# Attention in pairs of heads h and h+4, with q and k on 128 partitions and the order of every engine written out

## The chip, the cores and the metric

The program runs on one core of one Trainium2 chip. The metric is device time in microseconds (us), the median of several executions. Several chips were used; the kernel before took 374 to 383 us on them, so every version below is compared with runs of the kernel before on the same chip in the same rounds. A ratio is the mean time of one kernel's fast runs over the mean of the other's of the same rounds, so it is not quite the ratio of the medians that are quoted. A run counts as slow when it lies over 1.5% above the fastest of the same kernel.

## The reference

Sliding-window attention with a linear bias, then a mixture of eight experts in which each token goes to the expert named by its domain id. Sizes: 8 batches, 8 heads, 576 positions, head size 64, window 128; 4608 tokens of 512 features, experts 512 to 1024 to 512.

```python
def _attn_ref(q, k, v):                       # all (8, 8, 576, 64) float32
    scores = scale * np.matmul(q, k.transpose(0, 1, 3, 2))
    rel = pos[:, None] - pos[None, :]
    bias = slopes[:, None, None] * (-np.abs(rel))[None]
    mask = (rel >= 0) & (rel < 128)
    scores = np.where(mask, scores + bias[None], -1e9)
    # ... softmax over the last axis ...
    return np.matmul(attn, v)

def _moe_ref(x, domain_id, w1, w2):           # x (4608, 512), w1 (8, 512, 1024), w2 (8, 1024, 512)
    for e in range(8):
        m = domain_id == e
        out[m] = np.maximum(x[m] @ w1[e], 0.0) @ w2[e]

def reference(...):
    x = attn_out.transpose(0, 2, 1, 3).reshape(4608, 512)
    return _moe_ref(x, ...)
```

## The kernel before

The kernel has two parts. In attention, each batch is loaded, q and k are transposed on TensorE, scores are exponentiated on ScalarE, masked on VectorE, multiplied by v on TensorE, divided by their row sums on VectorE, and the finished 128-token rows are scattered by expert into a buffer in device memory (`x_srt`). A short routing step computes the scatter addresses from the domain ids. In the expert part (MoE), each expert's rows are loaded from `x_srt`, transposed and put through two matmuls. The MoE part cannot start before the last scatter of the last batch has landed, because any expert may own any row.

The parts that the change and the argument touch (cuts are marked with `...`):

```python
    PR, CR = 96, 6                                   # q, k: 96 partitions x 6 rows
    ...
    def load_w(e):                                   # 2 DMAs of one expert's weights, on GpSimd's queue
        w1e = wpl.tile([128, 4, FF], F16, name="w1e", tag="w1e")
        nc.gpsimd.dma_start(out=w1e, in_=moe_w1[e]...)
        w2e = wpl.tile([128, 8, DX], F16, name="w2e", tag="w2e")
        nc.gpsimd.dma_start(out=w2e, in_=moe_w2[e]...)
        return w1e, w2e
    ...
        def load_b(b):
            # q16, k16: [96, 8, 6*64]; q and k on GpSimd's queue (they are cast to fp16 on the way)
            for h0 in range(0, H, step):
                for (src, dst) in ((q, q16), (k, k16)):
                    nc.gpsimd.dma_start(out=dst[:, h0:h0 + step, :], in_=src[b, h0:h0 + step]...)
            # v: five tiles on SyncE's queue
            ...
        def stage_t(b, hp):                          # 2 heads: 12 transposes for q, 12 for k
            for (src, dst) in ((q16, qT), (k16, kT)):
                for c in range(CR):
                    for hh in range(2):
                        nc.tensor.transpose(pst[64*hh:64*hh+64, c*PR:(c+1)*PR],
                                            src[:, 2*hp+hh, c*D:(c+1)*D], ident[0:PR, 0:PR])
                ...
        def stage_s(b, h):                           # one head: 5 matmuls on one half of the rows
            d0 = 64 * (h % 2)
            for kt in range(NT):
                nc.tensor.matmul(ps[:, o:o + w], kT[d0:d0+64, kt*128:kt*128+128],
                                 qT[d0:d0+64, kt*128:kt*128+w], ...)
            # Exp on ScalarE, two masks on VectorE
            ...
        def stage_av(b, h, et):                      # 9 matmuls, reciprocal, one division
            ...
        def stage_out(b):                            # on GpSimd: 5 token copies, then 5 scatters
            ...
        for i, (b, h) in enumerate(units):
            et = stage_s(b, h)
            if i == 1:
                routing()
            if h == 2 and b + 1 < B:
                loaded[b + 1] = load_b(b + 1)
            if h == 2 and b == B - 1:
                ws.append(load_w(0))
            ...                                      # transposes two pairs ahead, v casts at h == 5
            if prev is not None:
                stage_av(*prev)
                if prev[1] == H - 1:
                    stage_out(prev[0])
            prev = (b, h, et)
    ...
        xs = [load_x(0, MT)]                         # MoE: expert 0's rows from x_srt, on SyncE's queue
        turn_x(*xs[0], MT)
        ws.append(load_w(1))
        for e in range(E):
            if e + 2 < E:
                ws.append(load_w(e + 2))
            ...
```

Here the framework's scheduler decides the order on each engine; the source order is only a wish. It moves the weights of the first three experts far forward, as the profile shows.

The softmax here doesn't subtract the row's maximum and nothing guards it: scores larger than these inputs give would overflow.

Of the kernel before, what the change touches and what calls it, by code (L numbers as in the profile page):

```python
# [10 lines left out]
F16 = mybir.dt.float16  # L11
F32 = mybir.dt.float32
I32 = mybir.dt.int32
I64 = mybir.dt.int64
ACTF = mybir.ActivationFunctionType
# [11 lines left out]
def kernel(  # L27
# [17 lines left out]
    PR, CR = 96, 6  # L45
    HP = H // 2
# [30 lines left out]
    cst = np.zeros((128, 64), np.float32)  # L77
    for (b, t), c in colof.items():
        cst[:, c] = b * S + t * 128 + np.arange(128)
# [11 lines left out]
    psX = ctx.enter_context(tc.tile_pool(name="psX", bufs=2, space=PSUM))  # L91
# [4 lines left out]
    cs = cpool.tile([128, 64], F32, name="cs")  # L96
    nc.sync.dma_start(out=mat, in_=mats_h.ap())
    nc.sync.dma_start(out=gm[:, :, 0:256], in_=gmask_h.ap())
    nc.sync.dma_start(out=cs, in_=cst_h.ap())
    ident = mat[:, 0, :]  # L100
    nc.gpsimd.tensor_copy(out=gm[:, :, 256:448], in_=gm[:, :, 0:192])
    nc.gpsimd.tensor_copy(out=gm[:, :, 448:512], in_=gm[:, :, 0:64])
# [9 lines left out]
    kTs = [cpool.tile([128, 640], F16, name=f"kT{i}") for i in range(3)]  # L112
    qTs = [cpool.tile([128, S], F16, name=f"qT{i}") for i in range(3)]
    ets = [cpool.tile([128, 1088], F16, name=f"et{i}") for i in range(3)]
# [13 lines left out]
    with tc.tile_pool(name="qk_pool", bufs=2) as qk_pool, \  # L128
         tc.tile_pool(name="v_pool", bufs=6) as v_pool, \
         tc.tile_pool(name="r_pool", bufs=4) as r_pool, \  # L130
         tc.tile_pool(name="rt", bufs=1) as rt:

        def load_b(b):
            q16 = qk_pool.tile([PR, H, CR * D], F16, name="q16", tag="q16")
            k16 = qk_pool.tile([PR, H, CR * D], F16, name="k16", tag="k16")
            step = 2 if b == 0 else 8
            for h0 in range(0, H, step):
                for (src, dst) in ((q, q16), (k, k16)):
                    nc.gpsimd.dma_start(
                        out=dst[:, h0:h0 + step, :],  # L140
                        in_=src[b, h0:h0 + step].rearrange(
                            "h (p c) d -> p h (c d)", p=PR))
            v32 = []
            for t in range(NT):
                n = SSZ[t]
                v32t = v_pool.tile([128, H, D], F32, name="v32", tag="v32")
                nc.sync.dma_start(  # L147
                    out=v32t[0:n],
                    in_=v[b, :, t * 128:t * 128 + n, :].rearrange("h p d -> p h d"))
                v32.append(v32t)  # L150
            return q16, k16, v32

        loaded = {0: load_b(0)}

        for t in kTs:
            nc.vector.memset(t[:, S:640], 0.0)
        for t in ets:
            nc.gpsimd.memset(t[:, 1024:1088], 0.0)
# [7 lines left out]
        def routing():  # L166
# [28 lines left out]
            pp = psX.tile([128, 512], F32, space=PSUM, name="pp", tag="x")  # L195
            nc.tensor.matmul(pp[:, 0:E * NCOL], mat[:, 1, :], cf, start=True, stop=True)
            pt = psX.tile([128, 512], F32, space=PSUM, name="pt", tag="x")
# [61 lines left out]
        qkT = {}  # L259
        scat = []  # L260

        def stage_t(b, hp):
            q16, k16, _ = loaded[b]
            i = b * HP + hp
            qT, kT = qTs[i % 3], kTs[i % 3]
            for (src, dst) in ((q16, qT), (k16, kT)):
                pst = psT.tile([128, 1024], F16, space=PSUM, name="pst", tag="t")
                for c in range(CR):
                    for hh in range(2):
                        nc.tensor.transpose(  # L270
                            pst[64 * hh:64 * hh + 64, c * PR:(c + 1) * PR],
                            src[:, 2 * hp + hh, c * D:(c + 1) * D],
                            ident[0:PR, 0:PR])
                o = dst[:, 0:S].rearrange("p (r c) -> p r c", c=CR)
                x = pst[:, 0:S].rearrange("p (c r) -> p r c", c=CR)
                if dst is qT:
                    nc.scalar.activation(o, x, ACTF.Copy)  # L277
                else:
                    nc.vector.tensor_copy(out=o, in_=x)  # L279
            qkT[b, hp] = (qT, kT)  # L280

        def stage_v(b):
            _, _, v32 = loaded[b]
            vb = vbs[b % 2]
            for t in range(NT):
                n = SSZ[t]
                nc.gpsimd.tensor_copy(out=vb[0:n, t, :, 0:D], in_=v32[t][0:n])  # L287

        def stage_s(b, h):
            hp, hh = h // 2, h % 2  # L290
            qT, kT = qkT[b, hp]
            d0 = 64 * hh
            ps = psS.tile([128, 1024], F32, space=PSUM, name="ps", tag="s")
            for kt in range(NT):
                o = kt * 256 if kt < 4 else 960
                w = min(256, S - kt * 128)
                nc.tensor.matmul(ps[:, o:o + w],  # L297
                                 kT[d0:d0 + 64, kt * 128:kt * 128 + 128],
                                 qT[d0:d0 + 64, kt * 128:kt * 128 + w],
                                 start=(kt in (0, 2)), stop=(kt in (1, 4)),  # L300
                                 skip_group_check=True)
            et = ets[(b * H + h) % 3]
            nc.scalar.activation(et[:, 0:1024], ps, ACTF.Exp, scale=QSCALE)  # L303
            nc.vector.tensor_tensor(  # L304
                out=et[:, 0:512].rearrange("p (a w) -> p a w", a=2),
                in0=et[:, 0:512].rearrange("p (a w) -> p a w", a=2),
                in1=_bcast(gm[:, h, 0:256], 1, 2), op=ALU.mult)
            nc.vector.tensor_tensor(out=et[:, 512:1024], in0=et[:, 512:1024],
                                    in1=gm[:, h, :], op=ALU.mult)
            return et  # L310

        def stage_av(b, h, et):
            vb, xt = vbs[b % 2], xts[b % 2]
            px = psX.tile([128, 512], F32, space=PSUM, name="px", tag="x")
            for qt in range(NT):
                for kt in (qt - 1, qt):
                    if kt < 0:
                        continue
                    o = kt * 256 if kt < 4 else 960
                    if kt < qt:  # L320
                        o += 128
                    nc.tensor.matmul(px[:, qt * 65:qt * 65 + 65],  # L322
                                     et[:, o:o + 128], vb[:, kt, h, :],
                                     start=(qt == 0), stop=(qt == NT - 1 and kt == qt),
                                     skip_group_check=True)
            pxv = px[:, 0:NT * 65].rearrange("p (t e) -> p t e", e=65)
            r = r_pool.tile([128, NT], F32, name="r", tag="r")
            nc.vector.reciprocal(out=r, in_=pxv[:, :, 64])  # L328
            nc.vector.tensor_tensor(out=xt[:, :, h * D:(h + 1) * D],  # L329
                                    in0=pxv[:, :, 0:D], in1=_bcast(r, 2, D),  # L330
                                    op=ALU.mult)

        def stage_out(b):
            xt = xts[b % 2]
            for t in range(NT):
                c = colof[b, t]
                nc.gpsimd.tensor_copy(
                    out=xt.bitcast(I32)[:, t, DX // 2:DX // 2 + 1],
                    in_=cs[:, c:c + 1])
            for t in range(NT):  # L340
                n, c = SSZ[t], colof[b, t]
# [6 lines left out]
                scat.append(sc)  # L348

        units = [(b, h) for b in range(B) for h in range(H)]  # L350
        pairs = [(b, hp) for b in range(B) for hp in range(HP)]
        stage_t(*pairs[0])
        stage_t(*pairs[1])
        stage_v(0)
        prev = None
        ws = []
        for i, (b, h) in enumerate(units):
            et = stage_s(b, h)
            if i == 1:
                routing()  # L360
            if h == 2 and b + 1 < B:
                loaded[b + 1] = load_b(b + 1)
            if h == 2 and b == B - 1:
                ws.append(load_w(0))
            if h % 2 == 0 and i // 2 + 2 < len(pairs):
                stage_t(*pairs[i // 2 + 2])
            if h == 5 and b + 1 < B:
                stage_v(b + 1)
            if prev is not None:
                stage_av(*prev)  # L370
                if prev[1] == H - 1:
                    stage_out(prev[0])
            prev = (b, h, et)
# [4 lines left out]
    with tc.tile_pool(name="xg_pool", bufs=2) as xg_pool, \  # L378
         tc.tile_pool(name="xT_pool", bufs=2) as xT_pool, \
         tc.tile_pool(name="h_pool", bufs=2) as h_pool, \  # L380
         tc.tile_pool(name="o_pool", bufs=6) as o_pool:
# [43 lines left out]
        def gemm2(hT, w2e, tk, n):  # L425
            for j in range(n):
                po = psX.tile([128, 512], F32, space=PSUM, name="po", tag="x")
# [16 lines left out]
        ws.append(load_w(1))  # L444
# [93 lines left out]
```

## Time and profile before

| | us |
|---|---|
| median of 3 runs (379.63 to 382.3) | 380.36 |
| span of the profiled execution (a slow run of 387.2) | 385.6 |
| first scatters of batches 0, 1, ... 7 start at | 59.3, 90.7, 104.5, 124.0, 145.9, 168.1, 189.5, 202.4 |
| last division of attention ends | 201.6 |
| first transposes of MoE | 214.4 |
| MoE to the end | 171.2 |

The view by stretches of time gives, for each stretch, the busy time of each engine with its instruction count, then the TensorE clock that the records show as granted (1.00 is full), the busy share of the DMA engines, and what they moved in GB/s. Kernel before:

```profile
core 0: us, PE busy (x) PEld busy (x) DVE busy (x) ACT busy (x) POOL busy (x), PEclk, DMA share, GB/s
40.00:80.00 40.00, 32.24 (x342) 20.23 (x339) 23.42 (x64) 17.70 (x20) 18.82 (x29) 1.00 1.14 202
120.00:180.00 60.00, 52.48 (x569) 33.17 (x566) 35.77 (x98) 28.46 (x33) 29.84 (x51) 1.00 0.63 121
200.00:220.00 20.00, 6.21 (x47) 4.59 (x48) 3.84 (x13) 0.70 (x1) 4.78 (x5) 1.00 0.36 118
220.00:300.00 80.00, 73.96 (x482) 44.41 (x481) 21.52 (x43) 21.83 (x31) 24.68 (x29) 0.98 0.82 175
```

Read it line by line. From 40 to 80 us the DMA engines are full (share 1.14): the early weights run beside v, q and k. From 120 to 180 us TensorE is busy 52.48 of 60 us while the DMA engines have room, so TensorE paces that stretch. At 200 to 220 us almost everything idles: this is the turn from attention to MoE. After it TensorE is the limit again (73.96 of 80 us).

### The profile page before, as it was taken

The numbers are of one execution on the slowest core, as the hardware profiler recorded it, in microseconds if no ns is written. First come the engines' busy times: TensorE is split into PE (matmuls) and PEld (weight loads), VectorE is DVE, ScalarE is ACT, GpSimd is POOL, SyncE is SP. The second block draws the span as 40 slices with busy tenths as digits, with TensorE's granted clock in tenths as the row PEclk, the third lists the DMA queues.
The fourth block names the chain that finished last, engine by engine and source line by source line (L and its number), as shares of the span: only waits on it lengthen the run. The fifth ranks groups of instructions, "written<-read, shape, count | busy, mean of one in ns | idle before, by whom it ended". The sixth has DMA issues, their size and how long they took to land.

```text
span 385.6 us, 6570 instructions
## 1 busy us (share of the span) xinstructions
PE 309.7 (80%) x2659; PEld 191.7 (50%) x2659; DVE 158.1 (41%) x404; ACT 131.5 (34%) x161; POOL 145.9 (38%) x227
## 2 busy tenths in 40 slices
PE   1718999469689797997960799798998969899992
PEld 1415665246356465664630565546564635556551
DVE  0408865534756565755670222130504022223221
ACT  2404554333545453544430132305050502323230
POOL 8540616605844727171224015041413315041423
PEclk9999999999999999999999999999999989999998
DMA  8999999999999958610012639598997969530302
GB/s 158 193 202 199 186 195 201 233 196 225 152 194 234 214 81 185 97 46 23 30 38 78 203 50 273 95 262 148 186 227 126 244 120 246 99 126 2 120 27 92
DMA packets 75386, 57.92 MB, mean 150 GB/s; under 512 B 39984, under 2 KB 67800, under 8 KB 75355
## 3 DMA queue, kind: packets, MB, share of 16 engines
q0 software_dynamic: 30176, 40.67, 53.5%
q1 hardware_dynamic: 45179, 16.82, 19.4%
q8 instruction: 21, 0.34, 0.4%
q14 instruction: 10, 0.08, 0.1%
HBM read 68.13 MB, written 16.61 MB: 220 GB/s over the span
## 4 chain that ended last, share of the span: by engine, by line
DMA 36%; PE 29%; issue 14%; POOL 8%; SPq 6%; DVE 3%; ACT 2%; another core or an unknown queue 1%; POOLq 1%; ACTq 0%; DVEq 0%
DMA out_dram<-osb,tk 18%; DMA v<-in_v_dram 15%; PE ps L297 9%; PE po L429 8%; PE px L322 6%; SPq L147 5%; PE pst L270 5%; POOL out_dram L433 3%; DMA k<-in_k_dram 3%; POOL x_srt L342 2%; ACT et L303 2%; PE pxT L395 1%; POOL vb L287 1%; DVE osb L432 1%
## 5 line engine op out<-in xcount | busy, mean ns | idle before, releaser
L297 PE MATMUL ps<-qT,kT 64*128 64x256 f16 (+2 forms) x320 | 79.6, 362 | 14.3 <-ACT et L303 13.0
L303 ACT ACTIVATE et<-ps 128x1024 f16<-128x1024 f32 x64 | 65.3, 1024 | 73.0 <-PE px L322 42.3
L413 ACT ACTIVATE hT<-ph 128x640 f16<-128x640 f32 x64 | 45.1, 704 | 127.0 <-PE ph L409 113.7
L429 PE MATMUL po<-w2e,hT 128*128 128x512 f16 x320 | 76.8, 390 | 0.0
L409 PE MATMUL ph<-xT,w1e 128*128 128x320 f16 x512 | 71.6, 300 | 0.0
L433 POOL DMA_INDIRECT out_dram<-osb,tk x40 | 39.7, 992 | 61.5 <-DVE osb L432 56.2
L409 PEld LDWEIGHTS <-w1e 128*128 128x128 f16 x512 | 50.3, 98 | 20.8
L322 PE MATMUL px<-vb,et 128*128 128x65 f16 x576 | 48.8, 243 | 1.6 <-DVE xt L329 1.2
L429 PEld LDWEIGHTS <-hT 128*128 128x128 f16 x320 | 31.5, 100 | 34.7 <-issue 3.6
L322 PEld LDWEIGHTS <-et 128*128 128x128 f16 x576 | 33.6, 126 | 29.1 <-issue 8.6
L432 DVE COPY osb<-po 128x512 f32<-128x512 f32 x40 | 27.7, 692 | 48.6 <-PE po L429 48.6
L342 POOL DMA_INDIRECT x_srt<-xt,dest_i x40 | 39.6, 991 | 20.2 <-issue 11.1
L297 PEld LDWEIGHTS <-kT 64*128 64x128 f16 x320 | 32.3, 119 | 25.8 <-issue 4.2
L287 POOL CAST vb<-v 128x512 f16<-128x512 f32 (+1 forms) x40 | 24.4, 637 | 52.9 <-DMA v<-in_v_dram 43.5
L328 DVE RECIPROCAL r<-px 128x5 f32<-128x5 f32 x64 | 12.3, 193 | 63.7 <-PE px L322 48.8
L395 PE MATMUL pxT<-mat,xg 128*128 128x128 f16 x160 | 15.7, 234 | 23.8 <-DMA xg<-x_srt 13.6
L277 ACT ACTIVATE qT<-pst 128x576 f16<-128x576 f16 x32 | 20.8, 649 | 38.4 <-PE pst L270 38.4
L270 PE MATMUL pst<-mat,q 96*64 96x96 f16 x384 | 22.9, 282 | 13.5 <-DMA q<-in_q_dram 12.3
L329 DVE TENSOR_TENSOR xt<-px,r 128x320 f16<-128x320 f32 x64 | 30.9, 483 | 1.5 <-DMA x_srt<-xt,dest_i 1.4
L304 DVE TENSOR_TENSOR et<-et,gm 128x512 f16<-128x512 f16 x64 | 30.2, 472 | 0.5 <-ACT et L303 0.4
L421 DVE COPY_PREDICATED tk<-used,xg 128x5 int32<-128x5 int32 x8 | 1.4, 172 | 67.6 <-POOL tk L420 54.8
L279 DVE COPY kT<-pst 128x576 f16<-128x576 f16 x32 | 24.0, 750 | 12.1 <-PE pst L270 12.1
(61 smaller groups left out, 168.0 us busy)
## 6 DMA issues: line engine op xcount, KB each, us to landing
v<-in_v_dram SPq DMA_DIRECT2D x32, 256.0 KB
w1e<-in_moe_w_dram POOLq DMA_DIRECT2D x8, 1024.0 KB
w2e<-in_moe_w_dram POOLq DMA_DIRECT2D x8, 1024.0 KB
xg<-x_srt SPq DMA_DIRECT2D x8, 680.0 KB
q<-in_q_dram POOLq DMA_DIRECT2D x7, 576.0 KB
k<-in_k_dram POOLq DMA_DIRECT2D x7, 576.0 KB
x_srt<-zr SPq DMA_DIRECT2D x1, 1088.0 KB
v<-in_v_dram SPq DMA_DIRECT2D x8, 128.0 KB
```

What stands on the lines that cost most here:

```text
L270: nc.tensor.transpose(pst[64 * hh:64 * hh + 64, c * PR:(c + 1) * PR], src[:, 2 * hp + hh, c * D:(c + 1) * D], ident[0:PR, 0:PR])
L297: nc.tensor.matmul(ps[:, o:o + w], kT[d0:d0 + 64, kt * 128:kt * 128 + 128], qT[d0:d0 + 64, kt * 128:kt * 128 + w], start=(kt in (0, 2)), s ...
L303: nc.scalar.activation(et[:, 0:1024], ps, ACTF.Exp, scale=QSCALE)
L304: nc.vector.tensor_tensor(out=et[:, 0:512].rearrange("p (a w) -> p a w", a=2), in0=et[:, 0:512].rearrange("p (a w) -> p a w", a=2), in1=_b ...
L322: nc.tensor.matmul(px[:, qt * 65:qt * 65 + 65], et[:, o:o + 128], vb[:, kt, h, :], start=(qt == 0), stop=(qt == NT - 1 and kt == qt), skip ...
L329: nc.vector.tensor_tensor(out=xt[:, :, h * D:(h + 1) * D], in0=pxv[:, :, 0:D], in1=_bcast(r, 2, D), op=ALU.mult)
L342: sc = nc.gpsimd.indirect_dma_start(out=x_srt, out_offset=bass.IndirectOffsetOnAxis(ap=dest_i[0:n, c:c + 1], axis=0), in_=xt[0:n, t, :], i ...
L409: nc.tensor.matmul(ph[:, s, 0:w], w1e[:, c, fc * 128:(fc + 1) * 128], xT[:, c, s * w:(s + 1) * w], start=(c == 0), stop=(c == 3))
L413: nc.scalar.activation(hT[:, fc, :].rearrange("p (s w) -> p s w", s=halves), ph[:, 0:halves, 0:w], ACTF.Relu)
L429: nc.tensor.matmul(po, hT[:, fc, j * 128:(j + 1) * 128], w2e[:, fc, :], start=(fc == 0), stop=(fc == 7))
L432: nc.vector.tensor_copy(out=osb, in_=po)
L433: sc = nc.gpsimd.indirect_dma_start(out=out, out_offset=bass.IndirectOffsetOnAxis(ap=tk[:, j:j + 1], axis=0), in_=osb, in_offset=None, bou ...
```

## The change

Intent: feed TensorE better. Heads h and h+4 are processed together; q and k lie on 128 partitions with 18 rows of 64 each, so a pair needs 18 transposes instead of 24 and a DMA packet is three times as long. The scores of the two heads go to the two row halves of TensorE, in alternation, so that they may overlap. Reciprocals and the second mask of a pair become one instruction each. And the order of each engine is the source order (`tc.manual_schedule()`), with the weights of experts 0 and 1 loaded in batches 6 and 7 instead of wherever the scheduler put them.

```diff
-    PR, CR = 96, 6
-    HP = H // 2
+    HQ = H // 2
+    CR = S // 32
+    CG = CR // 3
 ...
+         tc.tile_pool(name="psX", bufs=1, space=PSUM) as psX, \
+         tc.manual_schedule():
 ...
+        def load_qk(b):
+            q16 = qk_pool.tile([128, 2, CR * D], F16, name="q16", tag="q16")
+            k16 = qk_pool.tile([128, 2, CR * D], F16, name="k16", tag="k16")
+            step = CG * D if b == 0 else CR * D
+            for c0 in range(0, CR * D, step):
+                for (src, dst) in ((q, q16), (k, k16)):
+                    nc.gpsimd.dma_start(...)
 ...
+        load_qk(0)
+        nc.sync.dma_start(out=mat, in_=mats_h.ap())
+        load_v(0)
+        nc.sync.dma_start(out=gm[:, :, 0:256], in_=gmask_h.ap())
+        nc.sync.dma_start(out=cs, in_=cst_h.ap())
+        load_qk(1)
 ...
         def stage_s(b, h):
+            for kts in ((0, 1), (2, 3, 4)):
+                for kt in kts:
+                    for a in range(2):
+                        nc.tensor.matmul(ps[:, a, o:o + w],
+                            kT[64 * a:64 * a + 64, h, kt * 128:kt * 128 + 128],
+                            qT[64 * a:64 * a + 64, h, kt * 128:kt * 128 + w], ...)
 ...
         def stage_out(b):            # each token copy now directly before its scatter
 ...
+        for b in range(B):
+            for h in range(HQ):
+                ea, eb = stage_s(b, h)
+                mask_a(h, ea)
+                if b + 1 < B:
+                    for (src, j) in plan[h]:
+                        stage_t(b + 1, src, j)
+                mask_b(h, eb)
+                if b == 0 and h == 0:
+                    load_v(1)
+                    routing()
+                if prev is not None:
+                    stage_av(*prev)
+                    if h == 0:
+                        stage_out(b - 1)
+                prev = (b, h, ea, eb)
+                if h == 1:
+                    if b + 2 < B:
+                        load_qk(b + 2)
+                    if b + 2 >= B:
+                        ws.append(load_w(b + 2 - B))
+                if h == 2 and b + 1 < B:
+                    stage_v(b + 1)
+                    if b + 2 < B:
+                        load_v(b + 2)
         stage_av(*prev)
         stage_out(B - 1)
 ...
         xs = [load_x(0, MT)]
         turn_x(*xs[0], MT)
-        ws.append(load_w(1))
```

## The prediction

> **What bounds the kernel now.** Page: span 385.6 us (that profile ran slow; median 380.36). Attention's last division ends at 201.6 us (timeline). MoE transposes start at 214.4; from there TensorE is about 95% busy (stretches view), so the MoE part, some 170 us, is TensorE's; its body is unchanged.
> Attention has two regimes. To about 120 us the DMA engines are full (share 0.92 to 1.24 at about 190 GB/s, stretches view). Weights of three experts load at 22-100 us, beside v; batch 0 is scattered at 59 us. From 112 to 190 us TensorE paces it: 4.84 us for two heads (chain of waits), 24 transposes 1.24, scores 1.92, attention times v 1.22. A batch takes 20.4 us on average.
>
> **What changes per pair of heads.**
> - Scores: 10 matmuls on alternating row halves. The Trainium skill, "TensorEngine Tiling (Array Packing)", Key Properties, says different tiles load weights and multiply in parallel; before, the five of one head take 0.96 us on one half. Estimate 0.7-1.0 us a pair, saving about 1 us; no trace shows it yet.
> - Transposes: 18 instead of 24, each 128 instead of 96 columns: about 1.05, saving 0.2.
> - TensorE then needs about 3.3 us a pair, 13 a batch.
> - VectorE (2.93 us busy a pair) saves about 0.2 by merged reciprocal and mask; ScalarE stays at 2.7.
> - q, k: a third as many, longer packets. DMA need a batch: about 13-14 us.
> - Weights of experts 0 and 1 move to batches 6 and 7, expert 2 into MoE: frees about 25 us of early DMA time.
>
> **Why I don't expect the whole gain.** The order written out makes a loop. On POOL the q, k load for batch b+2 stands behind the scatters of b-1; these wait for the last attention-times-v of b-1; on TensorE that stands behind the first transposes of b+1, which wait for the q, k load issued one batch earlier. Its length, from the trace: transposes 0.75; k copy, mask, reciprocal and two divisions on VectorE 2.8; five scatters with a token copy each 7.3 (scatter 0.99 + 0.3 + copy 0.2); issue and landing of q and k 9.5 (one k load in this trace took 9.7). Sum about 20 us, against 13 of TensorE work. So from batch 2 on TensorE should wait 5-7 us in each batch.
> Start: TensorE's order puts routing's transpose before the rest of batch 0; the domain ids arrive behind v(1) and the zero fill at about 34-37 us (before: 26.9). Last attention-times-v of batch 0 at about 53 us, first late load about 70-72, four loop periods of 19-20, then two batches without late loads at 12-13: attention ends at about 175-180 us instead of 201.6. The last scatters cost 1-2 us more. MoE: same.
>
> **Prediction: 355 us, 8 in 10 between 337 and 368.** Faster by over 2%: 0.87; within 2%: 0.10; slower: 0.03.
>
> **What would show it.** Scores' five steps of a pair under 1.1 us in the timeline; TensorE idle 4-7 us per batch, released by the q or k DMA, at the first transposes of a batch, in batches 2 to 6; scatter groups 18-21 us apart; first routing transpose after 33 us; MoE from first transposes to end within 3 us of before.
>
> **What would make it wrong.** q, k landing in 5 us: no loop, batches of 13-14 us, about 330. Row halves not overlapping, or TensorE's clock falling in the waits: near 368.

## More of the kernel before

TensorE's waits, in the form: what it was about to do, what released it, total us, number of waits, longest. Kernel before:

```profile
PE pxT L395 <- DMA xg<-x_srt: 13.6, 1, 13.6
PE ps L297 <- ACT et L303: 13.0, 9, 3.3
PE pst L270 <- DMA q<-in_q_dram: 12.3, 2, 6.3
PE pd L187 <- DVE d L185: 8.6, 1, 8.6
PE pst L270 <- DMA k<-in_k_dram: 5.7, 4, 2.0
```

The largest, 13.6 us, is the turn; the fourth is the routing transpose (`pd`), which waits for the domain ids.

Two TensorE lines of the timeline of the kernel before: nine attention-times-v matmuls and the five score matmuls of one head. Columns: start, duration, engine, source line, what, shapes, count.

```profile
135.06 0.68 PE L322 MATMUL px<-vb,et 128*128 128x65 f16 x9
135.67 1.03 PE L297 MATMUL ps<-qT,kT 64*128 64x256 f16 x5
```

The turn in the timeline of the kernel before:

```profile
201.12 0.49 DVE L329 TENSOR_TENSOR xt<-px,r 128x320 f16<-128x320 f32 x1
...
207.49 0.91 POOL L342 DMA_INDIRECT x_srt<-xt,dest_i  x1 [0.30 <-issue]
210.05 0.94 SPq L385 DMA_DIRECT2D xg<-x_srt  x2
...
214.41 1.81 PE L395 MATMUL pxT<-mat,xg 128*128 128x128 f16 x13 [13.55 <-DMA xg<-x_srt]
```

The last division (201.12), the last of five scatters (issued 207.49), 2.6 us later the load of expert 0's rows may start (210.05), and 4.4 us after that TensorE has them.

## The result, and the profile after

The kernel got slower: median 392.24 us of 4 runs (392.02 to 393.71) against 381.33 of 4 runs of the kernel before (379.63 to 382.61); ratio of the fast runs 1.0297, 95% interval 1.0242 to 1.0352.

Stretches of the kernel after:

```profile
core 0: us, PE busy (x) PEld busy (x) DVE busy (x) ACT busy (x) POOL busy (x), PEclk, DMA share, GB/s
40.00:80.00 40.00, 20.78 (x341) 15.91 (x341) 29.61 (x74) 19.72 (x22) 11.54 (x17) 0.89 0.63 116
120.00:180.00 60.00, 34.32 (x574) 25.92 (x571) 43.81 (x86) 31.75 (x35) 33.52 (x53) 0.67 0.67 132
200.00:220.00 20.00, 1.44 (x12) 1.28 (x13) 1.02 (x3) 0.00 (x0) 0.00 (x0) 0.50 0.96 218
```

The aim was reached: TensorE's busy time at 120 to 180 us fell from 52.48 to 34.32 us. How much of this is the layout and how much the clock is not settled (see the third point of the last section). But the time did not follow it. And at 200 to 220 us the engines have next to nothing to do while the DMA engines are full (0.96, before 0.36).

TensorE's waits, kernel after:

```profile
PE pxT L419 <- DMA xg<-x_srt: 29.5, 1, 29.5
PE px L337 <- DVE xt L346: 23.8, 19, 4.0
PE pst L276 <- DMA q<-in_q_dram: 19.5, 5, 7.2
PE pd L196 <- DVE d L194: 19.4, 1, 19.4
PE pst L276 <- DMA k<-in_k_dram: 15.9, 9, 3.2
```

Four waits have grown: the turn (29.5 us, before 13.6), routing (19.4, before 8.6), q (19.5, before 12.3) and k (15.9, before 5.7).

TensorE in the timeline of the kernel after: a wait for k with the transposes behind it, scores at a low clock, and the same scores after the clock has risen:

```profile
101.78 0.85 PE L276 MATMUL pst<-mat,k 128*64 128x128 f16 x12 [3.19 <-DMA k<-in_k_dram]
...
103.67 1.03 PE L302 MATMUL ps<-qT,kT 64*128 64x256 f16 x10
...
109.10 0.61 PE L302 MATMUL ps<-qT,kT 64*128 64x256 f16 x10
```

Ten score matmuls of a pair take 0.61 us, or 1.03 after a wait; before, the five of one head alone took 1.03.

GpSimd in the timeline of the kernel after, one batch of the loop:

```profile
85.17 1.03 POOL L357 DMA_INDIRECT x_srt<-xt,dest_i  x1 [8.93 <-issue]
...
92.02 0.79 POOL L140 DMA_DIRECT2D q<-in_q_dram  x1
92.78 0.81 POOL L140 DMA_DIRECT2D k<-in_k_dram  x1
...
106.08 1.04 POOL L357 DMA_INDIRECT x_srt<-xt,dest_i  x1 [8.65 <-issue]
```

The five scatters of batch 1 hold GpSimd's queue from 85.17 to 92.02 (6.9 us). Only then are q and k of a later batch issued; k arrives at TensorE at 101.78 (the view above), 9.8 us later; after 4.3 us more of transposes, attention-times-v and division, the scatters of batch 2 start at 106.08. The sum, 20.9 us, is the period of the loop. The prediction had put its three parts at 7.3, 9.5 and 3.6 us.

The turn in the timeline of the kernel after:

```profile
189.19 0.96 POOL L120 DMA_DIRECT2D w2e<-in_moe_w_dram  x1
189.31 0.89 DVE L346 TENSOR_TENSOR xt<-px,r 128x320 f16<-128x320 f32 x2
...
190.26 0.78 POOL L117 DMA_DIRECT2D w1e<-in_moe_w_dram  x1
...
192.51 0.91 POOL L120 DMA_DIRECT2D w2e<-in_moe_w_dram  x1
...
198.22 0.92 POOL L357 DMA_INDIRECT x_srt<-xt,dest_i  x1 [0.28 <-POOL xt L354]
214.28 0.95 SPq L409 DMA_DIRECT2D xg<-x_srt  x2
...
218.48 1.71 PE L419 MATMUL pxT<-mat,xg 128*128 128x128 f16 x12 [29.46 <-DMA xg<-x_srt]
```

The last scatter is issued at 198.22, yet the load of expert 0's rows starts at 214.28, 16.1 us later (before: 2.6). Right before the scatters, on the same queue, stand the weights of expert 1 (`w2e` at 189.19, its `w1e` at 188.38), and between them those of expert 2 (190.26 and 192.51). The source has expert 2 in the MoE part; the scheduler still moved it between the written scatters. Two experts are 4.2 MB as the profile counts them, and at the 205 to 220 GB/s that the DMA engines show there, they need about 20 us (an estimate from these two numbers).

Since the first profile of the kernel before had caught a slow run, both kernels were profiled once more on one chip (runs 13 and 14 below, 381.75 and 394.49 us; each is a single run, but both times lie within 0.6% of the medians of the same kernels). Their spans, 380.1 and 392.8 us, split like this:

| stretch | before | after | difference |
|---|---|---|---|
| start to first scatter of batch 0 | 55.6 | 64.2 | +8.6 |
| from there to first scatter of batch 7 | 145.1 | 128.5 | -16.6 |
| first to last scatter of batch 7 | 5.1 | 6.9 | +1.8 |
| last scatter issued to first transposes of MoE | 6.9 | 20.6 | +13.7 |
| MoE to the end | 167.5 | 172.7 | +5.2 |
| sum | 380.1 | 392.8 | +12.7 |

So the change did gain 16.6 us in the batches. The start, the turn and the MoE part gave back 29.3.

### The profile page after: what moved, and what is told of

Read it like the earlier page. It is cut to its first block, busy times and chain, and to the rows that moved or that the text cites. A ratio compares the mean times of both kernels' runs of the same rounds, so it can differ in the third digit from the quotient of the medians.

```text
span 392.0 us, 6123 instructions
## 1 busy us (share of the span) xinstructions
PE 244.3 (62%) x2467; PEld 161.1 (41%) x2467; DVE 161.8 (41%) x334; ACT 125.8 (32%) x153; POOL 151.0 (39%) x222
## 5 line engine op out<-in xcount | busy, mean ns | idle before, releaser
L433 PE MATMUL ph<-xT,w1e 128*128 128x320 f16 x512 | 72.6, 303 | 0.0
L309 ACT ACTIVATE ea<-ps 128x1024 f16<-128x1024 f32 x32 | 32.9, 1028 | 77.9 <-PE ps L302 32.1
L419 PE MATMUL pxT<-mat,xg 128*128 128x128 f16 x160 | 15.9, 236 | 39.2 <-DMA xg<-x_srt 29.5
L316 DVE TENSOR_TENSOR ea<-ea,gm 128x512 f16<-128x512 f16 x64 | 33.9, 571 | 10.5 <-DMA gm<-c_gmask 7.3
L337 PE MATMUL px<-vb,ea 128*128 128x65 f16 x256 | 22.4, 221 | 24.6 <-DVE xt L346 23.8
L285 DVE COPY kT<-pst 128x768 f16<-128x768 f16 x24 | 22.9, 954 | 33.8 <-PE pst L276 33.7
L302 PE MATMUL ps<-qT,kT 64*128 64x256 f16 (+2 forms) x320 | 27.6, 310 | 12.3 <-DVE kT L285 10.3
L309 ACT ACTIVATE eb<-ps 128x1024 f16<-128x1024 f32 x32 | 32.9, 1029 | 0.0
L419 PEld LDWEIGHTS <-xg 128*128 128x128 f16 x160 | 12.7, 105 | 44.8 <-DMA xg<-x_srt 29.6
L276 PE MATMUL pst<-mat,q 128*64 128x128 f16 x288 | 17.8, 283 | 20.6 <-DMA q<-in_q_dram 19.5
L276 PE MATMUL pst<-mat,k 128*64 128x128 f16 x288 | 16.9, 268 | 21.9 <-DMA k<-in_k_dram 15.9
L283 ACT ACTIVATE qT<-pst 128x768 f16<-128x768 f16 x24 | 20.0, 832 | 26.4 <-PE pst L276 20.6
L337 PEld LDWEIGHTS <-ea 128*128 128x128 f16 x256 | 14.8, 114 | 30.2 <-DVE xt L346 27.9
```

The lines of the kernel that those rows point to most:

```text
L276: nc.tensor.transpose(pst[64 * a:64 * a + 64, c * 128:(c + 1) * 128], src16[:, a, (j * CG + c) * D:(j * CG + c + 1) * D], ident)
L309: nc.scalar.activation(e[:, :, 0:512], ps, ACTF.Exp, scale=QSCALE)
L316: nc.vector.tensor_tensor(out=x[:, a], in0=x[:, a], in1=_bcast(gm[:, h + HQ * a, 0:256], 1, 2), op=ALU.mult)
L337: nc.tensor.matmul(px[:, a, qt * 65:qt * 65 + 65], e[:, a, o:o + 128], vb[:, kt, h + HQ * a, :], start=(qt == 0), stop=(qt == NT - 1 and k ...
L419: nc.tensor.transpose(pst[:, c * 128:(c + 1) * 128], xg[:, j, c * 128:(c + 1) * 128], ident)
L433: nc.tensor.matmul(ph[:, s, 0:w], w1e[:, c, fc * 128:(fc + 1) * 128], xT[:, c, s * w:(s + 1) * w], start=(c == 0), stop=(c == 3))
```

## The experiments

The theory after seeing the traces has three parts. **Turn (Q in the expectations):** the last scatters stand in GpSimd's queue behind the weights, so MoE starts late. **Loop:** q and k stand in the same queue behind scatters, which sets about 20 us for a batch. **Start:** routing gets its domain ids late and holds VectorE. The rivals: for the turn, the bytes of the weights have to come in any case and delay MoE wherever they stand; for the loop, TensorE's low clock after each wait, or VectorE, sets the period; for all of it, the new layout is at fault and not the order. All sixteen runs gave correct results. Edits are against the kernel after unless said otherwise.

### 1. Weights behind the last scatters

```diff
-                    if b + 2 >= B:
-                        ws.append(load_w(b + 2 - B))
+                    if b + 2 == B:
+                        ws.append(load_w(0))
 ...
         stage_out(B - 1)
+        ws.append(load_w(1))
+        ws.append(load_w(2))
```

> Only edit to the changed kernel: the weights of experts 1 and 2 are issued after the scatters of the last batch instead of before and between them. Theory Q (queue order): the last scatters sat in the DMA queue behind 4.2 MB of weights; then the first MoE transposes come about 7-8 us after the last scatter is issued (19.3 us in the changed kernel), some 12-14 us earlier, and the time falls from 392 to 377-381 us. Rival B (bytes): the weights must be moved before or early in the MoE part anyway, and TensorE then waits for expert 1 or 2 instead; the time stays within 4 us of 392. Attention itself (last division at 190 us) is the same under both.

Measured: 391.84 us, ratio to before 1.0301 (1.0215 to 1.0388). No gain over the kernel after. The turn in the timeline of this kernel:

```profile
198.61 0.90 POOL L357 DMA_INDIRECT x_srt<-xt,dest_i  x1 [0.28 <-POOL xt L354]
...
201.24 14.66 SPq L411 DMA_DIRECT2D xg<-x_srt  x3
...
212.69 2.81 PE L421 MATMUL pxT<-mat,xg 128*128 128x128 f16 x20 [21.84 <-DMA xg<-x_srt]
```

What follows: the queue theory is right about the wait, since the load of the rows now starts 2.6 us after the last scatter (201.24 minus 198.61) instead of 16.1. But the rival is right too: the same 0.7 MB load then took 11.5 us, to 212.69, instead of 4.2 us, beside 4.2 MB of weights on the other queue. The Trainium skill's page "DMA: Bandwidth & Descriptors", section "Issuing engines are not separate DMA queues", says that loads of all issuing engines run on the same 16 engines and interleave; this trace agrees. A second wait for rows followed, and the first MoE matmuls met a low clock (0.76 at 220 to 230 us). Moving the weights by a few microseconds did not help; the later runs move them to where the DMA engines have more room.

### 2 and 3. The loop and the start, each alone

Run 2 issues q and k ahead of the scatters instead of behind them; run 3 loads the domain ids first.

```diff
                 mask_b(h, eb)
+                if h == 0 and b + 2 < B:
+                    load_qk(b + 2)
 ...
                 if h == 1:
-                    if b + 2 < B:
-                        load_qk(b + 2)
```

> Only edit to the changed kernel: the q, k load of batch b+2 is issued before the scatters of batch b-1 instead of behind them. Theory L (the loop through POOL's order): TensorE's waits for q and k at the first transposes of a batch (35 us in all) fall under 10 us, scatter groups come 13-15 us apart instead of 20.4, the last division comes at 150-158 us instead of 190, the granted clock goes up, and the time is 352-362 us (the weights still stand before the last scatters). Rival B (bytes): the DMA engines cannot bring q, k and v faster; groups stay 18-20 us apart and the time is over 380.

Measured: 373.63 us, ratio 0.9798 (0.9713 to 0.9883), which is 0.952 of the kernel after (0.9798 over 1.0297). Scatter groups start at 72.6, 87.3, 104.3, 117.8, 132.9, 147.5, 164.4 and 175.2 us: about 15 us apart instead of 20.4. The q and k waits fell from 35.4 to 11.2 us in total; in the waits of this run their lines are

```profile
PE pst L276 <- DMA q<-in_q_dram: 7.1, 3, 6.4
PE pst L276 <- DMA k<-in_k_dram: 4.1, 3, 2.5
```

So the loop through the queue did set the period, and VectorE, which does the same work in both kernels, did not. The gain was smaller than expected. One reason shows in the groups: the first one is 9 us later than without this edit. Most likely the earlier q and k loads fill the DMA engines while the domain ids are on their way (the routing wait grew from 19.4 to 29.1 us); this was not tested alone, but with the ids first as well (run 6) the first group starts at 50.1 us.

```diff
         load_qk(0)
         nc.sync.dma_start(out=mat, in_=mats_h.ap())
-        load_v(0)
+        # four loads of the domain ids, moved here out of routing()
+        nc.sync.dma_start(out=cs, in_=cst_h.ap())
         nc.sync.dma_start(out=gm[:, :, 0:256], in_=gmask_h.ap())
-        nc.sync.dma_start(out=cs, in_=cst_h.ap())
+        load_v(0)
         load_qk(1)
```

> Only edit to the changed kernel: domain ids, constants and masks are loaded ahead of v of batch 0 instead of behind v of batches 0 and 1 and the zero fill. Theory S (start): TensorE's wait of 19.4 us for the routing's transpose goes, the first scatter comes at 44-50 us instead of 63.6, everything behind moves with it, and the time falls by 12-18 us to 374-380. Rival B: the DMA engines have then only moved the same bytes in another order; the first scatter comes at 58 us or later and the time is over 386.

Measured: 379.53 us, ratio 0.9959 (0.9888 to 1.0029), 0.967 of the kernel after. The first scatters start at 50.0 us instead of 63.6, and the groups stay 20 to 21 us apart, as expected for a shift of the start alone.

### 4. The same layout, ordered by the scheduler

```diff
-         tc.tile_pool(name="psX", bufs=1, space=PSUM) as psX, \
-         tc.manual_schedule():
+         tc.tile_pool(name="psX", bufs=1, space=PSUM) as psX:
```

> Only edit to the changed kernel: the written order of engines is taken out, the scheduler orders the attention part too; the layout by pairs h, h+4, the longer q, k packets and the row halves stay. If the written order is what costs (theories Q, L, S together), this is faster than before: 340-372 us. If the pairs themselves cost the time (rival P: 72 transposes of 128 columns, one PSUM buffer for two heads' results), it stays at 385-395 us.

Measured: 372.21 us, ratio 0.967 (0.9552 to 0.9788). The profiled run of this kernel was a slow one, so only its order is used (the ratio rests on two fast runs): the scheduler puts all weights of experts 0 to 2 at 37 to 86 us, and the turn takes 6.9 us. This answers the third rival. The layout by pairs, long packets included, is 3% faster than the kernel before; writing out this order on top of it costs 6% (1.0297 over 0.967 is 1.065).

### 5. Weights in batches 2 to 4

```diff
-                    if b + 2 >= B:
-                        ws.append(load_w(b + 2 - B))
 ...
+                if h == 3 and b in (2, 3, 4):
+                    ws.append(load_w(b - 2))
```

> Only edit to the changed kernel: the weights of experts 0, 1, 2 are issued at the last step of batches 2, 3 and 4, in the middle of attention, where its DMA share is 0.45 to 0.78. Run e1 showed that behind the scatters the same weights take the time from the first load of sorted rows instead (11.4 us to land, not 4.2). Theory T (6.3 MB of weights cost some 10-15 us at the turn to MoE wherever they are issued near it, and nothing where the DMA engines have slack): last division stays at 188-193 us, the first MoE transposes come 7 us after the last scatter as before the change, and the time is 377-382 us. Rival: the weights slow the q, k loads in the loop by as much as they free at the turn; last division at 200 us or later, time 388 or more.

Measured: 389.3 us, ratio 1.0155 (1.0032 to 1.0277). A miss in size. The turn is cured: 6.8 us from last scatter to MoE instead of 20.3. But batches with weights in them take 22.7 to 23.2 us (DMA share 0.96 to 0.97 over 80 to 180 us), and attention's last division ends at 198.2 instead of 190.2. In this loop, too, weights cost time, most likely because the loads of q and k that TensorE waits for share the queue and the DMA engines with them.

### 6 and 7. All three edits, and score matmuls without alternation

Run 6 joins the edits of 2, 3 and 5. Run 7 adds an order of the score matmuls in which two or three of one row half follow each other.

```diff
-                for kt in kts:
-                    for a in range(2):
+                for a in range(2):
+                    for kt in kts:
```

> Three edits to the changed kernel together: q, k loads before the scatters (as e2, -18 us), domain ids and masks first (as e3, -12 us), weights in batches 2 to 4 (as e5, about -11 us). If these are three separate losses of order, they add: 348-356 us, or a little less, as e2 lost 9 us in the start that e3 removes: 340-350. If one cause (bytes) is behind all, they do not add: 362 or more.

> e6 with the scores of the first head of a pair all before those of the second, so that the row halves of TensorE do not alternate. If alternating halves overlap (prediction: ten matmuls 0.7-1.0 us against 1.92), the ten take some 1.6-2.0 us here at full clock. If TensorE is what bounds a batch in e6, 32 pairs then cost about 15-30 us more; if VectorE or DMA bounds it (VectorE was busy 17-18.6 of 20 us in e2), under 8 us more.

Measured: run 6 359.42 us, ratio 0.9408 (0.9334 to 0.9481), a little above what was expected, with batches of 17 to 22 us where the weights run. Run 7 360.08 us, ratio 0.9379 (0.9292 to 0.9466): the same. The score matmuls of a pair in run 7, from TensorE's timeline:

```profile
87.89 0.62 PE L302 MATMUL ps<-qT,kT 64*128 64x256 f16 x10
```

0.62 us against 0.61 with alternation, where 1.6 to 2.0 had been expected: a miss. It does not mean that the two halves do not overlap: a pair has 2048 columns of scores, and widening a full-array matmul from 320 to 512 columns costs 0.09 us (means 300 and 390 ns in the expert part of the kernel before), so 2048 columns one after the other would need about 0.96 us, an estimate from these two durations. The measured 0.61 is well below that. But the alternation in the source is not what makes the overlap.

### 8. TensorE kept warm

Twelve matmuls of 512 columns with unused results were added at the first pair of batches 2 to 6, where TensorE waits.

```diff
                 if b + 1 < B:
+                    if h == 0 and 2 <= b < B - 1:
+                        dm = psT.tile([128, 512], F32, space=PSUM, name="dm", tag="t")
+                        for _ in range(12):
+                            nc.tensor.matmul(dm, ident, gm[:, 0, :], start=True, stop=True)
                     for (src, j) in plan[h]:
```

> The changed kernel with twelve extra matmuls of 512 columns (results unused) at the point in batches 2 to 6 where TensorE waits for q, so that its clock does not fall (0.67 in those batches). Rival C (the fall of the clock is what lengthens attention): clock 0.85-1.0 there, batches 3 us shorter or more, time 375-380. Theory L (the loop of loads and scatters sets the length; of its links only some 1-1.5 us scale with the clock): batches 19-20.4 us, time 384-393.

Measured: 397.65 us, ratio 1.0415 (1.0362 to 1.0468). The stretch to compare with the kernel after (34.32 us busy at clock 0.67):

```profile
120.00:180.00 60.00, 36.51 (x574) 25.06 (x575) 39.83 (x81) 28.88 (x32) 34.74 (x53) 0.80 0.65 127
```

The clock rose to 0.80 here, and the scatter groups are still 20.0 to 21.3 us apart. After the extra matmuls the first transposes of a batch ran in 0.53 us instead of 0.85, and the next scatters still came no earlier. So the low clock does not set the period: that rival is refuted. Why this kernel came out slower than expected (384 to 393) is not shown.

### 9 and 10. Weights in the last three batches, alone and with the other edits

```diff
-                    if b + 2 >= B:
-                        ws.append(load_w(b + 2 - B))
 ...
+                if h == 0 and b in (6, 7):          # ahead of the scatters of b - 1
+                    ws.append(load_w(b - 5))
 ...
+                    if b == 5:                      # at h == 2, behind the last q, k load
+                        ws.append(load_w(0))
```

> Only edit to the changed kernel: the weights of experts 0, 1, 2 are issued after the last q, k load (in batch 5 behind its q, k load, in batches 6 and 7 ahead of the scatters), when nothing but scatters is left for the DMA engines in attention. This is the clean test of the turn to MoE: e1 moved the weights into the load of sorted rows, e5 into the loop of q, k loads. Theory T: the loop is untouched (last division 188-193 us), the last scatter no longer has 4.2 MB before it, first MoE transposes at 203-207 us instead of 218.5, time 376-380. Rival (any weights near the turn expose their bytes): transposes at 213 or later, time 386 or more.

> The three edits together, with the weights where e9 has them. In e6 the DMA engines were full (share 1.13-1.16) in batches 2 to 4, where the weights stood, and those batches took 19-21.6 us; batches without weights took 17. If DMA bytes set the length there: batches 16-17 us throughout, last division at 160-165 us (169 in e6), time 346-353. If the q, k loop or VectorE sets it: batches stay at 19-21, time 357 or more.

Measured: run 9 381.92 us, ratio 1.0213 (1.0123 to 1.0303) on a chip where the kernel before takes 374.29; the turn took 6.9 us, but attention ended at 195.8. Its GpSimd timeline shows one reason:

```profile
171.94 0.14 POOL L446 MEMSET tk<- 128x5 int32 x2 [8.77 <-DVE eb L321]
```

A fill of the MoE part (`tk`), which the scheduler had moved between the written scatters, waited 8.8 us for VectorE; its memory had belonged to attention (runs 15 and 16 give it memory of its own, and this wait is gone). The scatters of batch 5 stood behind it. "Written out" does not keep later instructions out. Run 10 (with the edits of 2 and 3): 340.35 us, ratio 0.9102 (0.9026 to 0.9178), with the first five groups 13.5 to 14 us apart and the last division at 153.0, better than expected (346 to 353 us, 16 to 17 us a batch).

### 11. q and k in thirds

Run 6 with q and k of every batch loaded in three parts each, so packets are a third as long and GpSimd issues six loads instead of two.

```diff
-            step = CG * D if b == 0 else CR * D
+            step = CG * D
```

> e6 with q and k loaded in thirds in every batch (pieces of 1536 bytes instead of 4608 in DRAM, the size before the change), so that the longer packets alone are undone. If longer packets are worth something where the DMA engines are full, batches grow by 1 us or more and the time by 6-12 us to 365-371; if the engines are limited by bytes, it stays within 3 us of e6 (359.4 on the chip where before took 383.2).

Measured: 369.3 us, ratio 0.9869 (0.978 to 0.9958), against 0.9408 for run 6. The two runs were made on different chips: by the ratios this is 4.9% more, by the times (369.3 against 359.42) 2.7%. Within these bounds it is what the long packets (or the fewer issues; the run does not part the two) are worth where weights run beside them.

### 12 to 14. The kernels before and after again

> The kernel before, unchanged, to have a profile of it in its usual state: span 379-382 us; attention as in the first profile (last division near 201 us); the MoE part 166-168 us if the 5 us of the slow profile lay there.

> The kernel before once more, to have its profile from the same chip as e14. The first profile of before was a slow run (387.2 us against a median of 380.4), so the accounting of before against after mixed states. Expected: last division 190-196 us, MoE part (first transposes to end) 166-168 us.

> The changed kernel on the same chip. Expected against e13: first scatter 5-7 us later, last scatter's issue 2-6 us later or equal, turn from last scatter to first MoE transposes 20 us against 6-7, MoE part longer by 2-6 us if expert weights or the cold start still cost there, equal if not.

Measured: the kernel before took 371.08 us on the faster chip and 381.75 on another, there with the kernel after at 394.49. Runs 13 and 14 are the table of stretches above. Run 12 shows that MoE takes the same there (166.8 us): the chips differ within attention. Some expectations missed: run 12 was expected at a span of 379 to 382 us and had 369.5; the last division of run 13 was expected at 190 to 196 and ended at 199.9; and against run 13, the first scatter of run 14 came 8.6 us later instead of 5 to 7, and its last one 6.2 us earlier instead of equal or later.

A ratio to the kernel before therefore shifts with the chip: runs 9 and 15, on different chips, took 381.92 and 381.4 us, almost the same, and have ratios of 1.0213 and 0.9951. The main comparisons also hold on one chip: run 15 (381.4) is 0.967 of the kernel after (394.49 in run 14), and runs 2 and 3 (373.63 and 379.53) ran in the rounds of run 1 (391.84), which has the time of the kernel after.

### 15 and 16. Weights in the last batches, and the fill's memory set apart

Runs 9 and 10 again, with the tile `tk` in a pool of its own, so that its fill waits for nobody.

```diff
+    tkpool = ctx.enter_context(tc.tile_pool(name="tkpool", bufs=2))
 ...
-            tk = xg_pool.tile([128, n], I32, name="tk", tag=f"tk{n}")
+            tk = tkpool.tile([128, n], I32, name="tk", tag=f"tk{n}")
```

> e9 mended. In e9 GpSimd sat idle 8.8 us before the scatters of batch 5, behind a fill of the MoE part that the scheduler had put there and whose memory came free only with the last q, k transposes; here that tile has memory of its own. Theory T: with that wait gone the loop and the last two batches are as in the changed kernel (last division 187-192 us), the first MoE transposes come at 200-205 us, and the time is 3.0-4.0% below the changed kernel's (0.99-1.00 of before; the changed kernel was 1.030). Rival: the weights in the queue still delay the last batches; 1.015 or more of before.

> e10 mended in the same way: the scatters of batch 5 lose their wait (17.8 us after those of batch 4 in e10, others 13.5), batch 7 no longer waits for its result buffer (8.1 us in e10). Expected 4-8 us below e10: 0.89-0.90 of before (e10 was 0.910). If the weights' bytes and not that wait held batches 5 to 7, it stays within 0.5% of e10.

Measured: run 15 381.4 us, ratio 0.9951 (0.9896 to 1.0005), which is 0.966 of the kernel after. The turn of run 15 in its timeline:

```profile
202.76 0.91 POOL L358 DMA_INDIRECT x_srt<-xt,dest_i  x1 [0.28 <-POOL xt L355]
...
209.50 2.81 PE L422 MATMUL pxT<-mat,xg 128*128 128x128 f16 x20 [14.52 <-DMA xg<-x_srt]
```

The load of expert 0's rows starts at 205.21, 2.5 us after the last scatter. From that scatter to the first transposes it is 6.7 us, 13.5 shorter than in the kernel after. The total moved by 3.4%, as expected, but attention ended at 196.2, later than expected (187 to 192). VectorE's timeline of run 15 names the place:

```profile
187.66 0.89 DVE L347 TENSOR_TENSOR xt<-px,r 128x320 f16<-128x320 f32 x2 [4.08 <-DMA x_srt<-xt,dest_i]
```

The first division of batch 7 waited 4.1 us for its output buffer, until the scatters of batch 5 had landed. They were issued at 168.3 to 174.5, behind the weights of experts 0 and 1 issued at 160 to 163 us. This fits the queue order a second time, at a place that has nothing to do with the turn: the scatters landed late behind the weights in front of them. It was not tested alone, and full DMA engines could hold them up as well.

Run 16: 346.3 us of five runs (343.21 to 348.15), ratio 0.9029 (0.8981 to 0.9076), the best together with run 10, and faster than the kernels before and after by 10% and 12%. It had been expected at 0.89 to 0.90. What the fill's wait itself was worth stays open, since runs 9 and 15, and 10 and 16, were made on different chips. One line of TensorE's waits in run 16:

```profile
PE pxT L421 <- DMA xg<-x_srt: 14.6, 1, 14.6
```

The turn is back near the 13.6 us of the kernel before; the waits for q and k came to 7.7 and 3.9 us. The three edits hardly interact: the ratios of runs 2, 3 and 15 to the kernel after (0.952, 0.967, 0.966) multiply to 0.889, and run 16 has 0.877. What is now largest in TensorE's waits is VectorE's division (26.5 us).

## Why the prediction was wrong

It said 355 us (337 to 368) and gave 3% to slower by over 2%; measured were 392.24. Point by point:

| step, as the prediction put it | predicted | measured |
|---|---|---|
| scores' five steps of a pair | under 1.1 us | 0.61, or 1.03 at a low clock |
| scatter groups apart | 18 to 21 us | 20.4 |
| TensorE waiting for q or k at first transposes | 4 to 7 us a batch | 35.4 us in all, 7.1 for each of five batches (run 14: 48.5, 9.7) |
| first routing transpose | after 33 us | 41.0 |
| first late load of q, k | 70 to 72 us | 71.7 |
| end of attention | 175 to 180 us | 190.2 |
| "The last scatters cost 1-2 us more" | 1 to 2 us | 15.8 (turn from last division, same chip: 12.7 before, 28.5 after) |
| "MoE: same" | within 3 us | +5.2 (same chip) |

**Right: the mechanism of the loop.** The prediction derived a period of about 20 us from durations in the trace of before, each part came out within 1 us, and run 2, which cuts this loop alone, confirmed it as the cause. The clock, which it named as a risk, did fall in the waits, but run 8 shows that it does not set the period.

**Wrong first of all: "The last scatters cost 1-2 us more".** The prediction had noticed that the weights move to batches 6 and 7 and booked it only as a relief of the early DMA time. It did not ask what stands behind them in the same queue at the end. Measured, the turn grew by 13.7 us counted from the last scatter, 15.8 from the last division. Runs 1 and 15 show why: the scatters land behind 4.2 MB of weights. Taking the weights out of that place, with nothing else changed but the fill's memory, is worth 3.4% (run 15 against the kernel after). The prediction also took it that expert 2 loads in MoE, as the source says; in fact its two loads were issued among the last scatters.

**Wrong second: the tail of attention.** "Four loop periods of 19-20, then two batches without late loads at 12-13: attention ends at about 175-180". The last late load went out at 153.4, and the two last batches did take 12.05 us each (first scatter of batch 5 at 166.1, last division at 190.2). But between them lies the way from that load to the scatters of batch 5, 12.7 us, which the sum left at no more than a few. This is an error of arithmetic inside a right model: 36.8 us from the last load to the end, where 26 to 31 were counted (175 to 180 less about 149, the first late load and four periods).

**Wrong third: the baseline.** The gain was counted from 201.6, the end of attention in a profile of a slow run; in run 13 (381.75 us) it is 199.9. That is about 2 us.

**MoE.** The +5.2 us are not settled. Of these, 2.9 lie in the second expert matmuls (means 379 and 389 ns in runs 13 and 14), but the slow profile of the kernel before also shows 390, and runs 1, 2 and 15 of the new layout show 379, so this may be the state of the run and not the change. In other versions of the new kernel MoE took 170.3 to 175.8 us, against 166.8 to 171.2 for the kernel before.

In sum, on the same chip: attention ended 8.3 us earlier instead of about 24, the turn took 15.8 us more instead of 1 to 2, and MoE 5.2 more instead of none: +12.7.

What stays open: whether length of packets or number of issues explains run 11, and what holds the last microseconds of MoE.

## What to carry to other kernels

When a change moves a large load, look at what follows it in the same DMA queue and who waits for that: here 4.2 MB in front of the last scatters cost 13.7 us, and moved behind them, beside the next load, they gained nothing (run 1, 391.84 us against 392.24). Draw the loop through the queue (load, transpose, multiply, scatter, next load) and put the loads for later batches ahead of the stores for earlier ones. Here the more efficient engine showed up in the time only after that: the same layout was worth 10% or cost 3%, by little more than the order.

## What the Trainium skill lacked or had wrong

- The Trainium skill's page "DMA: Bandwidth & Descriptors", sections "Queues, rings and completion order" and "Issuing engines are not separate DMA queues": they say that all queues run on the same 16 engines, which take packets from the rows in turn. Run 1 agrees: a 0.7 MB load on SyncE's queue took 11.5 us beside weights on GpSimd's, 4.2 without. The page lacks a figure for what a small DMA pays behind a bulk load of the same GpSimd queue: last scatter to next load 16.1 us here behind 4.2 MB, against 2.6 with nothing in front.
- "TensorEngine Tiling (Array Packing)", "Key Properties": different tiles work in parallel. The trace agrees (2048 columns of scores in 0.61 us, against about 0.96 estimated in series). The page leaves open whether the source must alternate; with two or three matmuls of one half in a row it was 0.62 us.
- "TensorE: Matmul & The Clock Gate", Part 1: two states, half and full clock, with a caveat that trace events of the clock can be unreliable. The granted clock reads 1.00 throughout the attention of the kernel before, yet nine attention-times-v matmuls take 0.68 us there, and in the kernel after the same nine fill 0.69 us when the clock reads 0.50 (from 103.05 us) and 0.44 us when it reads 1.00 (from 108.73 us). Before 60 us the kernel after, too, reads 1.00 while its ten scores take 1.03 us. So the kernel before seems to have multiplied at half rate through all of attention while the column said otherwise; this is read from durations alone and was not tested.
- "SBUF — State Buffer", "Who interferes with whom": a VectorE operation with two inputs in SBUF contends with a GpSimd operation that reads SBUF. The trace agrees: two masks (0.75 us in most places) took 2.59 us during the 3.31 us of v casts at 115 us in the kernel after. The page gives no such number for a loop in which both recur in each batch.
- None of the pages read speaks of the end of a phase, and of which loads to keep out of the queue there; this was worth 3.4% here (run 15 against the kernel after).
